# Two heads of K and V in one load: 64 partitions each, rows of 8 KB

## The chip, the core and the metric

The kernel runs on one core of a Trainium2 chip. The metric is device time in microseconds (us), from the start to the end of one execution. Three runs of the kernel before gave 230.35, 232.3 and 233.48 us. The profile that is read below is one more execution; it took 230.15 us, of which its instructions span 228.4 us.

## The reference

Two attention blocks and two feed-forward blocks follow each other, on eight sequences with one new token each. Both attention blocks use the same weights and the same cache; both feed-forward blocks share theirs.

```python
B, Sq, D = 8, 1, 448
Hq, Hkv, Sk, Dh = 16, 8, 4096, 256          # W = 1024: the last quarter of the cache
q = (x @ wq).reshape(B, Sq, Hq, Dh)
scores = einsum("bhqd,bhkd->bhqk", q, k[..., Sk-W:, :]) * Dh ** -0.5   # 2 query heads per K/V head
o = einsum("bhqk,bhkd->bhqd", softmax(scores), v[..., Sk-W:, :])
A(x) = o.reshape(B, Sq, Hq * Dh) @ wo
B(x) = silu(x @ w1) @ w2                     # F = 1792
x = x + A(layernorm(x));  x = x + B(layernorm(x))
x = x + A(layernorm(x));  x = x + B(layernorm(x))
```

All numbers are bf16. For one sequence and one K/V head the window is 1024 positions of 256 numbers, 512 KiB. Over 8 sequences, 8 heads and K and V that is 64 MiB (67.1 MB) of cache, read once and used by both attention blocks. The weights are 10.6 MB.

## The kernel before

All engines are programmed directly. Every piece of work is recorded as a task with what it reads and writes (`Plan.add`); the waits between engines are worked out from that. The order of tasks on PE, DVE, ACT and POOL is not found by the program: it is written out as lists of task numbers (`ORDER`, at the top). SP, which issues nearly all loads, takes its tasks in the order in which the program records them.

**Loads.** The cache goes into 30 slots (`slots`, R = 30), each 128 partitions of 4 KiB: one K or V head. `load_kv` (L490) issues one transfer for one head; the head's 1024 positions are laid out so that partition p holds eight positions in a row, so each of the 128 partitions gets one run of 4 KiB of memory. `pump` (L978) records as many loads as there are free slots; a slot's next load waits until the tasks that last read the slot are done. At the start, SP issues x, the weight of the queries (`wq`, in rows of 8 KiB for its three large parts), the first eight K heads, then `w2` and `wo`, the first eight V heads, `w1`, and then K and V of one sequence after the other. The output leaves in two stores: seven rows for the first seven sequences (L928), and the last row cut in four (L965).

**One sequence, first attention.** DVE turns each K head in place, in 32 by 32 blocks of 4-byte words (`transposes`, L632, run at L639): in one instruction for the first four heads (`WIDE`), in two for the others. `scores` (L642, matmuls at L656) multiplies four heads at once, each on its own 32 rows of PE, for two groups of four heads (`k2`). The query operand `qbd` is spread out over 256 columns for each group: by POOL for the first attention (`q_blocks1`, L626), and by PE and ACT for the second one (L846, L850). `softmax` (L662) takes the maximum (L673), shares it between the row groups (L674, L675, L677), takes the exponential on ACT (L688), rearranges it on PE (L690) and turns it on DVE (L692). `products` (L699, matmuls at L703) multiplies with V head by head, each time with 4 rows fewer, so that each later head overwrites the rows that it owns. The last two heads (`LATE`) are multiplied apart (`products_late`, L712), since their V arrives last. `o_turn` (L725 to L733) scales and turns the result, `wo_rows` (L754) multiplies with `wo`, and `fold` brings the row back into columns.

**The rest of a sequence.** `chain` does the feed-forward block (L544 w1, L818 w2) and the queries of the second attention (L833, L838, L839, L846, L850). `attend2` and `values2` do the second attention from the same slots and so free them. The next sequence's first attention is interleaved with it. The second feed-forward block is done for seven sequences at once in `final_rows`, and for the last one in `final_last`; its helper constants (L874 to L880) are made there. `warm` (L781) puts filler matmuls on PE, whose result nobody reads.

Of the kernel before, what the change touches and what calls it, by code (L numbers as in the profile page):

```python
# [14 lines left out]
        "196 69 74 86 87 88 89 197 198 92 136 94 199 137 138 139 148 149 161 150 200 151 201 154 202 203 157 204 205 "  # L15
        "159 206 207 208 209 228 229 211 213 225 226 231 227 233 235 214 237 215 240 216 242 217 218 248 249 219 275 "
        "276 251 257 220 254 259 264 262 325 277 279 280 278 281 282 221 312 222 313 267 314 315 287 288 223 318 289 "
        "321 290 224 326 327 328 329 323 330 331 343 297 344 333 300 340 341 351 342 346 335 352 353 302 348 354 355 "
        "350 356 357 371 374 376 336 358 409 382 383 368 410 411 385 388 393 391 398 396 412 413 414 415 416 446 447 "
        "448 449 401 337 338 421 452 422 423 424 459 455 339 431 460 461 462 463 434 457 464 465 484 476 477 467 436 "  # L20
        "469 473 474 479 475 481 485 486 483 487 504 509 507 488 489 490 491 515 516 501 542 543 518 521 524 526 531 "
        "529 544 470 546 547 548 549 545 534 579 554 580 581 582 555 556 557 471 585 564 472 588 592 567 593 594 595 "
        "596 590 617 618 597 598 569 609 619 610 600 606 607 612 608 620 621 614 616 602 637 640 642 622 623 675 624 "
        "676 648 649 634 603 604 651 654 657 659 664 662 677 725 679 680 681 682 678 712 713 667 714 715 687 688 689 "
        "718 605 690 721 697 726 727 728 729 730 723 731 742 700 733 743 750 751 752 753 735 739 740 745 741 754 702 "
        "747 755 749 756 757 770 773 775 808 736 767 781 782 809 810 784 787 792 790 797 795 812 813 814 815 811 800 "
        "845 846 847 848 820 821 737 822 851 738 823 854 830 856 859 860 861 833 862 875 863 864 883 876 866 858 884 "
        "885 886 872 887 878 873 874 880 888 882 835 889 903 890 906 908 868 900 941 914 915 942 917 869 920 925 923 "
        "930 928 943 944 945 946 947 948 978 979 980 981 933 870 984 871 953 954 987 955 956 992 993 994 995 989 996 "
        "997 1008 991 963 999 1001 1009 966 1005 1006 1011 1007 1013 1016 1017 1002 1015 968 1018 1036 1041 1039 "  # L30
        "1019 1020 1021 1022 1023 1047 1048 1033 1074 1075 1050 1076 1053 1056 1058 1063 1061 1077 1078 1079 1066 "
        "1080 1081 1084 1085 1086 1087 1105 1106 1107 1108 1090 1111 1118 1093 1003 1004 1114 1142 1143 1144 1119 "
        "1116 1120 1121 1122 1123 1124 1145 1134 1146 1147 1126 1095 1135 1131 1132 1137 1133 1139 1148 1128 1149 "
        "1141 1129 1154 1157 1151 1159 1197 1198 1165 1166 1199 1200 1168 1130 1171 1176 1174 1181 1179 1196 1202 "
        "1250 1224 1184 1225 1226 1227 1237 1238 1239 1240 1211 1208 1233 1251 1246 1252 1253 1235 1254 1259 1248 "
        "1260 1261 1262 1256 1213 1264 1258 1266 1218 1268 1219 1271 1274 1284 1276 1221 1285 1286",
    "dve":
        "37 28 39 43 34 26 36 46 42 25 38 24 5 13 4 54 7 32 44 40 18 30 33 6 22 27 45 50 11 57 31 29 9 49 52 70 15 "
        "19 72 51 73 132 75 58 134 3 84 80 81 59 76 60 141 82 48 135 77 133 10 53 83 140 143 35 16 55 146 144 142 78 "
        "20 17 145 90 91 85 93 14 174 12 21 175 56 147 169 184 185 152 41 170 155 162 163 179 158 160 47 8 189 180 "  # L40
        "190 271 272 236 273 241 243 245 23 247 274 252 309 258 304 310 260 261 311 307 308 306 305 265 266 316 319 "
        "322 295 324 298 301 405 406 407 370 408 375 303 377 379 381 438 441 439 386 442 444 394 392 395 445 443 440 "
        "399 400 450 453 429 456 432 435 458 538 539 503 540 510 508 514 437 512 541 573 571 519 575 576 525 527 528 "
        "574 532 577 572 533 578 583 562 586 565 589 568 591 671 672 570 673 636 674 641 643 645 647 705 706 708 652 "
        "707 711 658 660 661 704 710 709 665 666 716 719 695 722 698 724 701 804 805 703 806 769 807 774 776 778 780 "
        "837 839 838 785 840 842 793 791 794 843 844 798 799 841 849 852 828 855 831 857 834 937 938 939 902 836 940 "
        "907 909 911 913 971 970 973 918 975 977 926 924 927 972 974 976 931 932 982 985 988 961 990 964 967 1070 "
        "1071 1035 1072 1042 1040 969 1046 1044 1073 1098 1100 1051 1099 1101 1057 1059 1060 1097 1064 1065 1103 "
        "1102 1104 1088 1109 1091 1112 1094 1115 1117 1096 1186 1153 1158 1188 1160 1189 1162 1187 1193 1164 1169 "
        "1190 1191 1177 1192 1194 1175 1195 1178 1182 1183 1204 1206 1228 1229 1207 1230 1231 1241 1242 1243 1244 "  # L50
        "1234 1247 1236 1209 1249 1212 1214 1215 1217 1269 1275 1277 1279 1280 1282 1283 1222 1287",
    "act":
        "2 71 164 165 166 167 171 172 176 153 177 168 178 181 182 156 183 186 187 191 188 192 210 212 230 193 232 "
        "234 238 95 173 244 246 250 253 255 263 268 317 320 296 332 299 334 345 347 349 372 378 380 367 384 369 387 "
        "389 397 402 451 454 430 433 466 468 478 480 482 505 513 511 500 517 520 502 522 530 535 584 563 587 566 599 "
        "611 601 613 615 638 644 646 633 650 635 653 655 663 668 717 720 696 699 732 744 734 746 748 771 766 777 779 "
        "783 786 788 768 796 801 850 853 829 832 865 877 867 879 881 904 899 910 912 916 901 919 921 929 934 983 986 "
        "962 998 965 1000 1010 1012 1014 1037 1045 1043 1032 1049 1034 1054 1052 1062 1067 1089 1110 1092 1113 1125 "
        "1127 1136 1138 1140 1150 1155 1152 1161 1163 1167 1201 1170 1172 1180 1203 1205 1185 1232 1245 1255 1263 "
        "1257 1265 1216 1267 1220 1272 1270 1278 1281",  # L60
    "pool":
        "0 1 79 130 131 239 269 270 256 404 403 373 390 536 506 523 537 669 639 656 670 802 772 789 803 905 935 936 "
        "922 1068 1069 1038 1055 1156 1173 1210 1273",
# [160 lines left out]
def bass_interleave_layers__sliding_block_cached__dense_activation_silu__decode_kernel(  # L224
# [5 lines left out]
    H = HD // DH  # L230
# [12 lines left out]
    R = 30  # L243
    WIDE = (0, 1, 2, 3)
    LATE = 2
    WARM = (8, 12, 5, 4, 4, 4, 4, 4, 3)
# [15 lines left out]
    slots = [sb(f"slot{i}", [P, 2048], BF16) for i in range(R)]  # L262
# [43 lines left out]
    def QB(i, k2):  # L306
        return [("qbd", i, k2, q) for q in range(4)]

    PT = [QB(i, 0) for i in range(2)]
    EK = [QB(i, 1) for i in range(2)]  # L310
# [22 lines left out]
    def dma(fn, writes, n_bytes, key, reads=(), rate=407e3, via="sp"):  # L333
# [3 lines left out]
    SCR2 = slots[R - 2][:, :]  # L337
    SCRATCH = {R - 1: ["xrow", "xh", "sq8", "sqh8", "st8", "q1T", "sel", "sel_f", "quad_f", "lsel_f", "nm8", "rh8"] +
               [("sums", "w2", g) for g in range(4)] + [("sums", "wo", g) for g in range(8)], R - 2: ["big8", "junk"]}
# [13 lines left out]
    junk = SCR2[:, 512:512 + D]  # L353

# [19 lines left out]
    const(qbd[1][:], 0.0, [("pad", 1)] + QB(1, 0) + QB(1, 1) + QM, dur=0.2)  # L374
# [17 lines left out]
    for k2 in range(2):  # L392
        dve(lambda e, k2=k2: e.tensor_copy(
            view(perm[:], 8 * (1 - k2), [(32, 4), (2, 4), (1, 2)]),
            view(ident[:], 96 + 8 * (1 - k2), [(1, 4), (-32, 4), (4, 2)])),
            ["ident", "perm0"], [("perm", k2)], 0.12, -1, "init")
    PERM = [("perm", 0), ("perm", 1)]
    for q in range(4):
# [5 lines left out]
        0.2, -1, "init")  # L404
    dve(lambda e: e.tensor_copy(sel_o[:], sel_f.rearrange("p (n a) -> p a n", a=2)), ["sel_f"], ["sel_o"], 0.1, -1,
        "init")
    dve(lambda e: e.tensor_reduce(quad_f, ident[:].rearrange("p (g n) -> p g n", n=4), AX.X, ALU.add), ["ident"],
        ["quad_f"], 0.2, -1, "init")
    dve(lambda e: e.tensor_copy(quad[:].rearrange("p (g n) -> p g n", n=4), quad_f.unsqueeze(2).broadcast_to([P, 32, 4])),
        ["quad_f"], ["quad"], 0.2, -1, "init")  # L410
# [79 lines left out]
    def slot_key(s):  # L490
        return [("slot", s, 0), ("slot", s, 1)]
# [129 lines left out]
    def qdata(i, k2):  # L621
        return view(qbd[i][:], 8 + 256 * k2, [(8, 32), (4, 2), (1, 4)])
# [354 lines left out]
    def pump():  # L977
        while n_load[0] < len(seq) and (n_load[0] < cap[0] or n_load[0] >= R and seq[n_load[0] - R] in freed):  # L978
# [4 lines left out]
            if x == (0, "k", 7):  # L983
                load_w2()
                load_wo()
# [113 lines left out]
```

## Time and profile before

| What | Value |
|---|---|
| Median of three runs | 232.3 us (230.35 to 233.48) |
| The profiled execution, its time and its span | 230.15 us, 228.4 us |
| PE, DVE, ACT, POOL busy | 173.0, 157.2, 71.4, 22.8 us |
| All transfers | 78.21 MB in 22,681 packets, mean 342 GB/s |
| Of these, the queue that SP issues to | 22,486 packets, 77.32 MB |
| Loads of K and of V | 64 and 64, of 512 KB each |
| Median from issue to landing, K and V | 8.3 and 10.1 us |
| Clock granted to PE | full throughout |

The page shows the busy time by engine, then the span cut in 40 slices (a digit is the busy share of a slice in tenths), the transfers, the chain of work that ended last, and the costliest groups of instructions by line. The DMA rows give the mean busy share of the core's 16 DMA engines and the rate that they moved. A "packet" is one run of bytes that a DMA engine moved, or the small write by which it reports that its part of a transfer has ended.

### The profile page before, as it was taken

Reading aid. Unit: us, or ns where it says so; the run is one execution under the profiler, and the core shown is the slowest. Engines: PE = TensorE matmul, PEld = TensorE weight load, DVE = VectorE, ACT = ScalarE, POOL = GpSimd, SP = SyncE. Lnnn points to the kernel's source line nnn. Section 1 sums busy time; section 2 is a strip of 40 time slices with the busy share of each in tenths; the row PEclk is TensorE's granted clock in tenths of the full one; section 3 lists DMA queues with packets and bytes.
Section 4 is the critical chain, followed back from the end, with each engine's and each line's share of the span. In section 5 each row is a group of like instructions: output and inputs, shape, how many; then the busy total and the mean of one; then the engine's idle time right before and its main releaser. Section 6 shows DMA issues by size and latency. Waiting matters only on the chain.

```text
span 228.4 us, 8452 instructions
## 1 busy us (share of the span) xinstructions
PE 173.0 (76%) x3779; PEld 94.1 (41%) x3779; DVE 157.2 (69%) x369; ACT 71.4 (31%) x218; POOL 22.8 (10%) x41
## 2 busy tenths in 40 slices
PE   0020737357878989999898987888989999999894
PEld 0010623123444455445444644554445445544662
DVE  6238989878792797389459837974895589314644
ACT  2000080633302341432324142414332431353341
POOL 1000130000200210101010101110120200000020
PEclk9999999999999999999999999999999999999999
DMA  6999999999999999999999999999999999700000
GB/s 175 413 406 407 382 380 395 411 414 417 405 400 369 377 408 403 396 408 407 406 406 408 402 378 411 408 392 395 410 409 385 380 408 406 307 3 3 0 6 1
DMA packets 22681, 78.21 MB, mean 342 GB/s; under 512 B 2279, under 2 KB 5302, under 8 KB 22262
## 3 DMA queue, kind: packets, MB, share of 16 engines
q1 hardware_dynamic: 22486, 77.32, 86.6%
q8 instruction: 29, 0.48, 0.9%
q10 hardware_dynamic: 160, 0.36, 0.6%
q14 instruction: 6, 0.05, 0.1%
HBM read 77.67 MB, written 0.01 MB: 340 GB/s over the span
## 4 chain that ended last, share of the span: by engine, by line
PE 46%; DVE 31%; DMA 10%; ACT 6%; issue 4%; SPq 2%; DVEq 0%; ACTq 0%
DVE slot L639 12%; DMA slot<-in_A_k_cache_dram 10%; PE bank L656 10%; PE bank L703 7%; DVE slot L472 7%; PE pair L754 6%; PE bank L781 2%; PE pair L833 2%; ACT ot L760 2%; PE bank L675 2%; PE bank L846 2%; PE bank L712 2%; PE bank L833 2%; PE pair L529 2%; PE pair L818 1%
## 5 line engine op out<-in xcount | busy, mean ns | idle before, releaser
L639 DVE STREAM_TRANSPOSE slot<-slot 128x512 uint32<-128x512 uint32 (+1 forms) x96 | 80.2, 866 | 7.0 <-DMA slot<-in_A_k_cache_dram 6.8
L656 PE MATMUL bank<-slot,qbd 128*16 128x256 bf16 (+1 forms) x1024 | 40.9, 285 | 5.1 <-DVE slot L639 2.0
L703 PE MATMUL bank<-slot,qbd 128*24 128x512 bf16 (+6 forms) x416 | 31.1, 393 | 3.5 <-DVE qbd L692 3.3
L656 PEld LDWEIGHTS bank<-slot,qbd 128*16 128x16 bf16 (+1 forms) x1024 | 23.2, 87 | 16.7 <-ACT qbd L850 4.0
L781 PE MATMUL bank<-wq_sb,cols 128*1 128x512 bf16 x192 | 19.6, 416 | 13.9 <-DMA wq_sb<-in_A_wq_dram 13.9
L776 POOL TENSOR_TENSOR fcols<-fcols 128x1 f32<-128x1 f32 x17 | 9.4, 554 | 106.4 <-ACT fcols L774 94.5
L754 PE MATMUL pair<-wo_sb,q1s 128*1 128x449 bf16 x288 | 17.2, 353 | 1.1 <-DVE wo_sb L475 0.8
L850 ACT ACTIVATE qbd<-bank 128x256 bf16<-128x256 f32 x16 | 6.1, 384 | 33.5 <-PE bank L846 33.5
L725 ACT ACTIVATE ot<-bank,q1s 128x512 bf16<-128x512 f32 (+1 forms) x16 | 10.8, 673 | 16.4 <-PE bank L703 11.1
L626 POOL TENSOR_TENSOR qbd<-q1s,fcols 128x256 bf16<-128x256 bf16 x16 | 9.7, 614 | 59.7 <-PE bank L712 42.4
L703 PEld LDWEIGHTS bank<-slot,qbd 128*24 128x24 bf16 (+6 forms) x416 | 9.7, 92 | 11.1 <-DVE qbd L692 4.2
L692 DVE STREAM_TRANSPOSE qbd<-bank 128x256 bf16<-128x256 bf16 x17 | 8.0, 473 | 8.2 <-PE bank L690 7.9
L673 DVE TENSOR_REDUCE q1s<-bank 128x1 f32<-128x256 f32 x15 | 6.3, 423 | 8.1 <-PE bank L656 8.0
L472 DVE TENSOR_REDUCE slot<-wo_sb 128x6 f32<-128x2688 bf16 x4 | 11.8, 2948 | 0.1
L781 PEld LDWEIGHTS bank<-wq_sb,cols 128*1 128x1 bf16 x192 | 4.2, 82 | 15.4 <-issue 13.9
L674 ACT ACTIVATE q1s<-fcols,q1s 128x4 f32<-128x4 f32 x15 | 4.4, 296 | 18.7 <-DVE q1s L673 18.7
L675 PE MATMUL bank<-q1s,quad 128*128 128x4 f32 x30 | 6.0, 269 | 4.7 <-ACT q1s L674 4.5
L598 PE MATMUL pair<-slot,wq_sb 128*128 128x16 bf16 x128 | 3.6, 174 | 7.5 <-DVE slot L591 7.5
L833 PE MATMUL pair<-wq_sb,q1s 128*1 128x256 bf16 x256 | 8.9, 275 | 0.3 <-DVE q1s L765 0.3
L688 ACT ACTIVATE qbd<-bank,q1s 128x256 bf16<-128x256 f32 x15 | 7.1, 472 | 6.3 <-DVE q1s L677 6.0
L712 PE MATMUL bank<-slot,qbd 128*7 128x256 bf16 (+7 forms) x192 | 8.6, 283 | 0.6 <-DVE qbd L692 0.6
L833 PE MATMUL bank<-wq_sb,q1s 128*1 128x512 bf16 x128 | 8.8, 390 | 0.0
(168 smaller groups left out, 244.6 us busy)
## 6 DMA issues: line engine op xcount, KB each, us to landing
slot<-in_A_k_cache_dram SPq DMA_DIRECT2D x64, 512.0 KB, 8.3
slot<-in_A_v_cache_dram SPq DMA_DIRECT2D x64, 512.0 KB, 10.1
wo_sb<-in_A_wo_dram SPq DMA_DIRECT2D x4, 896.0 KB, 14.6
wq_sb<-in_A_wq_dram SPq DMA_DIRECT2D x3, 1024.0 KB, 8.0
w_sb<-in_B_w_dram SPq DMA_DIRECT2D x1, 1568.0 KB, 19.8
w_sb<-in_B_w_dram SPq DMA_DIRECT2D x1, 1344.0 KB, 17.2
wq_sb<-in_A_wq_dram ACTq DMA_DIRECT2D x1, 256.0 KB, 3.5
wq_sb<-in_A_wq_dram SPq DMA_DIRECT2D x1, 256.0 KB, 4.1
```

Source lines behind the costliest of these rows:

```text
L472: dve(lambda e, rows=rows, s=s: e.tensor_reduce(s, rows[:, :, R0:M1].rearrange("p c (a n) -> p c a n", a=2), AX.X, ALU.add, negate=True), ...
L626: pool(lambda e, k2=k2: e.tensor_tensor(qdata(0, k2), q1s[:, b, 64 * k2:64 * k2 + 64].rearrange("p (n r) -> p n r", r=2).unsqueeze(3) .bro ...
L639: dve(lambda e, v=v: e.transpose(v, v), keys, keys, 0.15 + n / 2 / 950, b, ("KW%d" if n > 1024 else "KT%d") % k)
L656: fns.append(lambda e, w=w, j=j, kv=kv, cb=cb, par=par: e.matmul(sc[32 * j:32 * j + up_to, 0:256], w, kv, start=(cb == 0 and par == 0), st ...
L675: pe(lambda e: e.matmul(mx, quad[:], mq, start=True, stop=True, skip_group_check=True), [K[4], "quad"], bk(LB[n]), 0.2, b, "mx%d" % L)
L703: pe([lambda e, t=t: e.matmul(bank[ob][32 * t:32 * t + m, :], pT_sb[L][:, 64 * t:64 * t + m], v[:, 512 * t:512 * t + 512], start=True, sto ...
L712: pe([lambda e, t=t, a=a: e.matmul(o[32 * t:32 * t + m, :], pT_sb[n][:, 64 * t + a:64 * t + a + m], v[:, 512 * t + DH * a:512 * t + DH * a ...
L725: act(lambda e: e.activation(o_t, src[1], ACTF.Copy, scale=sm[b][:, 4 * L + 3:4 * L + 4]), bk(src[0]) + [("sm", b, L, 3)], okey, 0.62, b, ...
L754: fns.append(lambda e, i=i, w=w, c0=c0: e.matmul(bank[XB][32 * (i % 4):32 * (i % 4) + 1, c0:c0 + D + 1], oT[:, oT_col(i):oT_col(i) + 1], w ...
L776: pool(lambda e: e.tensor_tensor(rhalf, var4, nhalf, ALU.pow), ["var4", "nhalf"], ["rhalf"], 0.54, b, "pow" + name)
L781: pe([lambda e, i=i: e.matmul(bank[OB[0]][32 * i:32 * i + 1, :], zero_b, wq_sb[:, 512 * i:512 * i + 512], start=True, stop=True, tile_posi ...
L833: pe([lambda e, j=j, c=c, qh=qh, k2=k2, h=h, n=n: e.matmul(qh[32 * j:32 * j + 1, :], xbt[b][:, xcol(c, k2):xcol(c, k2) + 1], view(wq_sb[:] ...
```

## The change

K and V heads are loaded in pairs. A slot is now 128 partitions of 8 KiB, and there are 15; head 2j lies on partitions 0 to 63, head 2j + 1 on partitions 64 to 127, and each partition holds sixteen positions of its head in one run of 8 KiB. One transfer of 1 MiB fills a slot. Its source is written as a pattern of its own with three dimensions, slowest first: 2 heads (one head's cache apart), 64 rows, 4096 numbers. The last V pair of the last sequence comes in two transfers, each with one half of every row.

What follows from the layout: `qbd` needs 128 columns for a group instead of 256; the scores of one head pair come from two halves of a slot; the constants that share the maximum and rearrange the exponentials change (`perm`, `quad`, `sel4`, `lsel`); `products` accumulates over the two halves of a slot, with 8 rows fewer from pair to pair. The number of turns, score matmuls and product matmuls stays the same. The initial queries are spread by one set of 16 matmuls and two DVE copies instead of 32 matmuls, a DVE and an ACT copy. In the last sequence's second attention, the maximum is shared through PE as in the other sequences instead of by two turns on DVE; the constants of `final_rows` are made in the second sequence; `final_last` scales by the layernorm's factor at the end rather than before w2. All four `ORDER` lists are new.

```diff
...
-    R = 30
-    WIDE = (0, 1, 2, 3)
+    R = 15
+    NP = HKV // 2
+    WIDE = (0, 1)
     LATE = 2
+    SLOT = 4096
...
-    slots = [sb(f"slot{i}", [P, 2048], BF16) for i in range(R)]
+    slots = [sb(f"slot{i}", [P, SLOT], BF16) for i in range(R)]
...
-    def load_kv(s, cache, b, kvh):
+    def load_kv(s, cache, b, j, apart):
+
         extra = SCRATCH[s] if s in SCRATCH and s not in first_use else []
         first_use.add(s)
-        dma(lambda e: e.dma_start(slots[s][:, :].rearrange("p (u d) -> p u d", d=DH),
-                                  cache[b, kvh, S0:SK, :].rearrange("(p u) d -> p u d", p=P)),
-            slot_key(s) + extra, W * DH * 2, "slot%d" % s)
+        a = cache[b, 2 * j, S0:SK, :]
+        step = SLOT // 2 if apart else SLOT
+        for h in range(SLOT // step):
+            src = bass.AP(a.tensor, a.offset + h * step, [[SK * DH, 2], [SLOT, 64], [1, step]])
+            dma(lambda e, h=h, src=src: e.dma_start(slots[s][:, h * step:(h + 1) * step], src),
+                slot_key(s, h if apart else None) + extra, P * step * 2, "last%d" % h if apart else "slot%d" % s,
+                rate=407e3 if apart else 417.7e3)
...
     def qdata(i, k2):
-        return view(qbd[i][:], 8 + 256 * k2, [(8, 32), (4, 2), (1, 4)])
+        return view(qbd[i][:], 8 + 128 * k2, [(8, 16), (4, 2), (1, 4)])
...
-                    a = 16 + 256 * k2 + (j * 8 + cb * 2 + par) * 8
+                    a = 16 + 128 * k2 + (j // 2 * 8 + cb * 2 + par) * 8
                     w = q[:, a - up_to:a]
-                    kv = slots[slot_of[b, "k", 4 * k2 + j]][:, :].rearrange(
+                    kv = slots[slot_of[b, "k", 2 * k2 + j // 2]][:, 2048 * (j % 2):2048 * (j % 2) + 2048].rearrange(
                         "p (u cb jj par) -> p cb par u jj", u=8, cb=4, par=2)[:, cb, par, :, :]
...
+        dve(lambda e: e.tensor_reduce(mneg, x, AX.X, ALU.max, negate=True), bk(sb), [K[0]], 0.41, b, "max%d" % L)
         if part is None:
             act(lambda e: e.activation(mq, sel4, ACTF.Copy, scale=mneg), [K[0], "sel4"], [K[4]], 0.2, b, "mq%d" % L)
...
         else:
...
-            dve(lambda e: e.transpose(mt, mt), [("mt", n)], [("mt", n)], 0.21, b, "mT")
...
+            dve(lambda e: e.tensor_scalar(mq, sel4, mneg, None, op0=ALU.mult), [K[0], "sel4"], [K[4]], 0.12, b, "mqd")
+        pe(lambda e: e.matmul(mx, quad[:], mq, start=True, stop=True, skip_group_check=True), [K[4]] + QUAD,
+           bk(LB[n]), 0.2, b, "mx%d" % L)
...
-    def products(b, L, kvh, ob):
+    def products(b, L, j, ob):
 
-        v = slots[slot_of[b, "v", kvh]]
-        m = 4 * (HKV - kvh)
-        pe([lambda e, t=t: e.matmul(bank[ob][32 * t:32 * t + m, :], pT_sb[L][:, 64 * t:64 * t + m],
-                                    v[:, 512 * t:512 * t + 512], start=True, stop=True, tile_position=(0, 32 * t),
-                                    skip_group_check=True) for t in range(4)],
-           slot_key(slot_of[b, "v", kvh]) + PT[L], bk(ob), 0.055, b, "PV%d" % L)
+        v = slots[slot_of[b, "v", j]]
+        m = 8 * (NP - j)
+        for h in range(2):
+            pe([lambda e, t=t, h=h: e.matmul(
+                bank[ob][32 * t:32 * t + m, :], pT_sb[L][:, 64 * t + 32 * h:64 * t + 32 * h + m],
+                v[:, 2048 * h + 512 * t:2048 * h + 512 * t + 512], start=(h == 0), stop=(h == 1),
+                tile_position=(0, 32 * t), skip_group_check=True) for t in range(4)],
+               slot_key(slot_of[b, "v", j], h) + PT[L], bk(ob), 0.055, b, "PV%d" % L)
...
-            qs = bank[lb][:, 256:512]
+            qs = bank[lb][:, 256:384]
...
-            act(lambda e, qs=qs, k2=k2: e.activation(qbd[1][:, 8 + 256 * k2:264 + 256 * k2], qs, ACTF.Copy), bk(lb),
-                QB(1, k2) + QM * k2, 0.42, b, "qbd%d" % k2)
+            act(lambda e, qs=qs, k2=k2: e.activation(qbd[1][:, 8 + 128 * k2:136 + 128 * k2], qs, ACTF.Copy), bk(lb),
+                QB(1, k2), 0.28, b, "qbd%d" % k2)
...
-    seq = [(b, t, k) for b in range(NB) for t in "kv" for k in range(8)]
+    seq = [(b, t, k) for b in range(NB) for t in "kv" for k in range(NP)]
     n_load = [0]
-    cap = [R - 2]
+    cap = [R - 1]
...
-            freed.update((b, "k", 4 * k2 + j) for j in range(4))
+            freed.update((b, "k", 2 * k2 + j) for j in range(2))
             pump()
...
-            for kvh in range(HKV):
-                products(b, 1, kvh, OB[1])
-                freed.add((b, "v", kvh))
+            for j in range(NP):
+                products(b, 1, j, OB[1])
+                freed.add((b, "v", j))
             pump()
```

## The prediction

> **What bounds the kernel now.** I read the page's slices first, for the transfers.
>
> ```profile
> DMA  6999999999999999999999999999999999700000
> GB/s 175 413 406 407 382 380 395 411 414 417 405 400 369 377 408 403 396 408 407 406 406 408 402 378 411 408 392 395 410 409 385 380 408 406 307 3 3 0 6 1
> DMA packets 22681, 78.21 MB, mean 342 GB/s; under 512 B 2279, under 2 KB 5302, under 8 KB 22262
> ```
>
> The 16 DMA engines are at 90% or more from slice 2 to slice 34, that is from about 6 to 195 us; then they stop, and the last 28 us are work on data that is there. So two things set the time: the stream of 67.1 MB of K and V, and the tail behind its last load. Next I read the waits and the chain, to see whether the engines' work is far from the stream.
>
> ```profile
> SPq L496 <- PE bank L656: 59.5, 12, 8.9
> ...
> DVE slot L639 <- DMA slot<-in_A_k_cache_dram: 6.8, 9, 1.8
> ```
>
> SP waits 59.5 us in all for slots that the score matmuls still hold, at most 8.9 us at a time, and DVE waits only 6.8 us in all for K. Loads and work are nearly balanced, about 21 us for a sequence (67.1 MB / 8 at 408 GB/s is 20.6 us). Work that gets shorter gains little alone; transfers that get slower are seen at once, since they have no reserve.
>
> Then I looked at stretches of the start (columns: length, busy time of PE, PEld, DVE, ACT, POOL, the clock, the DMA engines' share, GB/s). From 6 to 12.5 us nearly all packets are rows of 8 KiB, those of `wq`; from 14 to 22 us they are mostly K in rows of 4 KiB.
>
> ```profile
> 6.00:12.50 6.50, 0.00 (x0) 0.00 (x0) 1.25 (x10) 0.00 (x0) 0.00 (x0) 1.00 1.00 417
> 14.00:22.00 8.00, 1.28 (x21) 0.68 (x17) 6.29 (x21) 0.23 (x1) 0.00 (x0) 1.00 1.03 408
> ...
> 150.00:190.00 40.00, 36.06 (x806) 19.83 (x810) 28.60 (x60) 13.97 (x42) 4.59 (x8) 1.00 1.02 397
> ```
>
> So rows of 8 KiB move at 417 GB/s instead of 408: one engine's sixteenth is 26.1 instead of 25.5 GB/s, 314 ns for a row of 8 KiB and 161 ns for one of 4 KiB. That is what the longer rows can bring, if all 16 engines carry them.
>
> Do they? The new source pattern is written slowest dimension first as 2 x 64 x 4096; so far each load's pattern began with 128 or 64 rows on both sides. The trace has three transfers that begin with fewer than 16: x (8 rows), and the stores of 7 and of 4 rows. I read the packets of the first 2.0 us and of 226.3 to 228.4 us, where only these three run:
>
> ```profile
> DMA packets 16, 0.01 MB, mean 4 GB/s; under 512 B 8, under 2 KB 16, under 8 KB 16
> ...
> DMA packets 22, 0.01 MB, mean 3 GB/s; under 512 B 15, under 2 KB 22, under 8 KB 22
> ```
>
> x has 8 rows of 896 B and just 8 small packets beside them. The stores have 7 rows of 896 B, 4 rows of 224 B, and 11 small packets: 7 + 4. The whole page says the same: 141 loads with 64 or 128 rows at 16 reports each are 2,256, plus 8 + 7 + 4, plus the four rows of 224 B, is 2,279, the page's count under 512 B to the last one. With 16 reports for every transfer it would be 2,308. So a transfer is cut along its outermost dimension into shares that report singly, 16 of them at most, and with fewer rows only so many. Cut that way, a source that begins with 2 makes two shares, and a load of 1 MiB runs on two DMA engines, 512 KiB (64 rows of 8 KiB) on each.
>
> In the three short transfers both sides begin with the same number; here the source begins with 2 and the slot with 128, and no row shows which decides. I take the smaller: a cut in more shares than 2 would have to go through the source's second dimension. The Trainium skill ("DMA: Bandwidth & Descriptors", "Why a DMA increments its semaphore by 16 and not by 1") says that the engines are the largest number up to 16 that divides the outermost counts of both sides, which is 2 here, and that they are then the lowest-numbered ones, load after load; for 8, 7 and 4 the trace agrees, for 2 against 128 no run so far shows it. By that page's 27 GiB/s for an engine, 33.55 MB on each of two would take an estimated 1157 us, and my sum below would be about 1220.
>
> **The sum.** Each of two engines carries 63 loads x 64 rows of 8 KiB, 4,032 x 314 ns = 1267 us, and of the last pair, loaded in halves of a row, 2 x 64 rows of 4 KiB, 128 x 161 ns = 20.6 us: 1288 us. The weights (10.6 MB) still go over all 16, and these two carry their sixteenth, 0.66 MB, in the same order: at 23.8 GB/s (slices 4 and 5, 382 and 380 GB/s) 28 us. Before the first of it 3 us pass. Behind the last load the tail stays: the last V head's first matmul is at 200.68 us, the span ends at 228.4, so 28 us. The execution is 1.75 us longer than its span (230.15 against 228.4). 1288 + 28 + 3 + 28 + 2 = **1349 us**. The profiled execution is 1% below the median of 232.3 us, which does not matter at this size; a difference under about 2% can't be told from no change here.
>
> Both ends: the stream's slowest long stretch, 397 GB/s, gives 24.8 GB/s for an engine, 33.55 MB / 24.8 = 1353 and 1414 in all. Two engines alone may each be faster than a sixteenth of what 16 move together; the nearest row is the best single microsecond of the `wq` loads (10 to 11 us), 451 GB/s or 28.2 for one, hence 1190 and 1251 in all. I take 26.1, the row with the same row length.
>
> Could anything starve the two engines further? A load takes 20 us, a pair of K is turned and used in a few us, and SP is up to 15 loads ahead; a slot that waits for its sequence to end has others queued before it. So nothing else counts but the tail.
>
> **The other edits**, each with its cover. For a sequence, 161 us of loading stand beside some 21 us of work, so all of it is hidden but for the tail; the prices without that cover matter to the first rival.
> - DVE's turns (L639, 64 x 683 and 32 x 1234 ns) keep number and shape. Product matmuls (L703) keep their number, and cost 392 to 399 ns with 12 to 32 rows alike: 0.
> - `qbd` at 128 columns: POOL (L626, 614 ns x 16) was waited for only 1.5 us in all by PE. ACT (L850) goes from 384 ns to somewhere between 178 (128x8, L733) and 384, PE's spread (L846) from 227 ns for 64 columns to between 167 (one column, L529) and 227. Taken at the middle, 0.1 + 4 x 0.03 us, 16 times: 3.5 us, of which PE's idle time for L850 (4.0 us in all) lets perhaps 1 us through.
> - Setup: six more copies of 0.18 us on DVE, which is free from 8 to 14 us (PE first has `wq` at 13.9); 16 fewer q matmuls (189 ns overlapped, 0.6 us for 16) and no ACT copy: -0.6 us once.
> - Ten small DVE operations for `final_rows` (0.06 to 0.17 us, some 1.2 us) move into the second sequence, where DVE is at 70 to 90%: at most +1.2, and they leave a stretch (201 to 211 us) in which DVE was mostly idle: 0.
> - Tail: the maximum by PE costs 0.15 + 0.39 + 0.16 us instead of 0.21 + 0.19 + 0.21 (+0.1), the two L801 of 0.22 us go, one lies on the path (-0.2), and ACT's new copy runs beside PE's w1 matmuls: 0 in all. What would be late next there is PE at L959, which waits for the same tanh.
> - SP issues 65 loads instead of 128 at 0.43 us (L496); a pattern with three dimensions may cost 0.3 (L928) to 0.6 (L965). Queued behind them in SP are only more loads and, at the end, the two stores; at one issue in 20 us nobody waits.
>
> **Rivals.**
> 1. *All 16 engines carry each load* (the slot's 128 partitions decide the cut; the point from which it turns is that the smaller count does not rule). Then 67.1 MB take 160.9 us at 417 instead of 164.5 at 408: -3.6, and -1 from `qbd` and setup: 230.15 - 4.6 = 225.5 us, 221 to 234 with what the new orders may lose or gain. For it: slices at 408 are full, so a faster row would show. Against it: the count of reports. The Trainium skill's "Rules for kernel authors" on the same page asks for 1 MiB and 128 partitions per transfer for most bandwidth, which speaks for this one; the 417 GB/s row agrees for `wq`, whose pattern begins with 128. 12%: 7 faster, 5 within 2%.
> 2. *Two engines for a load, but other ones for the next.* Eight loads in flight then fill all 16; each takes 20.6 us (64 x 314 ns, and its report) instead of 1.3. The first K and the last V come 19 us later: 230 + 2 x 19, less what overlaps, about 260 us. For it speaks only that the page has no view by engine. 4%.
> 3. *16 engines, but the larger slots starve the stream.* A slot is free only when both heads are done; half a slot is 1.29 us at 408 GB/s, and 16 phases of K or V would lose up to 20 us, about 240 us taken at half. Against it: waits of up to 8.9 us for slots left the DMA row full. 2%.
>
> **How the numbers follow.** Two engines: 82%. Its bounds, 1250 to 1415, hold nearly all of it, about 8 in 10 of everything, so the range ends there and leaves the rivals out. Slower by over 2%: 82 + 4 + 2 = 88%; within 2%: 5%; faster: 7%.
>
> **What will show it.** Right: a DMA row with 1 (two of 16 busy is 0.13), about 52 GB/s in nearly all slices; some 65 x 14 = 910 fewer small packets than 16 reports a load would make; K's time to landing of 100 us or more; PE and DVE at 10 to 20% and waiting for loads; a tail of some 28 us. Wrong at its first step if the DMA row stays at 9 and 417 GB/s; wrong in size if two engines alone move clearly more or less than 52 GB/s.

## The result

The changed kernel takes **1339.93 us** (median of four runs, 1338.72 to 1341.01) where the kernel before took 231.57 us beside it (230.35 to 233.48): **5.78 times as long** (95% interval 5.74 to 5.83). The profiled execution took 1338.72 us, its span 1336.9 us. Some executions of a kernel are a few per cent slower than its others: the medians below count them all, the ratios with their intervals only the fast ones, and the profiles of the runs with 16 first, with two transfers for a slot and with 14 slots are of slow ones.

The page's slices of the kernel after, each now 33 us long, and its count of packets:

```profile
PE   0103021120221201121022201022021020113007
...
PEclk9999995565555656655565655555565565556558
DMA  4152121111111111111111111111111111111110
GB/s 150 53 151 86 56 84 53 53 53 53 53 53 53 53 53 53 53 53 53 53 53 54 53 52 53 53 53 53 52 53 53 53 53 53 53 53 53 53 53 6
DMA packets 12699, 78.20 MB, mean 58 GB/s; under 512 B 361, under 2 KB 3384, under 8 KB 4216
```

The 16 DMA engines, at 9 tenths before, show 1 and 53 GB/s from the seventh slice to the last but one. The higher slices at the start hold the weights. The 361 small packets add up to the last one: 65 K and V loads with 2 reports each are 130, the 13 weight loads with 16 are 208, x and the two stores 8 + 7 + 4 = 19, and the four rows of 224 B.

Three stretches (columns: length, busy time of PE, PEld, DVE, ACT, POOL, the clock granted to PE, the DMA engines' share, GB/s):

```profile
14.00:22.00 8.00, 0.60 (x4) 0.12 (x4) 0.00 (x0) 0.00 (x0) 0.00 (x0) 1.00 0.13 53
200.00:700.00 500.00, 81.04 (x1250) 36.48 (x1247) 48.27 (x101) 19.84 (x62) 5.93 (x13) 0.55 0.13 53
...
1310.00:1337.00 27.00, 23.24 (x581) 13.62 (x573) 9.86 (x36) 9.25 (x31) 3.14 (x4) 0.98 0.01 3
```

A share of 0.13 is two of sixteen, from the first K load (14 to 22 us, 408 GB/s before) to the last V, but for the weights. Only the last 27 us are dense work again. The waits of the same kernel (in all, times, longest) say who pays: DVE waited 6.8 us for K before and now 756.2, and PE 319.9 for V.

```profile
DVE slot L662 <- DMA slot<-in_A_k_cache_dram: 756.2, 31, 89.5
...
PE bank L719 <- DMA slot<-in_A_v_cache_dram: 319.9, 21, 18.8
```

### The profile page after: what moved, and what is told of

It is laid out like the page before. It is cut to its first block, busy times and chain, and to the rows that moved or that the text cites. A ratio compares the mean times of both kernels' runs of the same rounds, so it can differ in the third digit from the quotient of the medians.

```text
span 1336.9 us, 8373 instructions
## 1 busy us (share of the span) xinstructions
PE 233.1 (17%) x3767; PEld 109.0 (8%) x3767; DVE 157.1 (12%) x375; ACT 69.9 (5%) x218; POOL 19.3 (1%) x41
## 4 chain that ended last, share of the span: by engine, by line
another core or an unknown queue 66%; SPq 13%; PE 8%; DMA 7%; DVE 4%; issue 1%; ACT 1%; POOL 0%; DVEq 0%
SPq L517 8%; DMA slot<-in_A_k_cache_dram 4%; DMA slot<-in_A_v_cache_dram 3%; DVE slot L662 3%; PE bank L679 2%; SPq L464 2%; SPq L470 1%; SPq L458 1%; PE bank L719 1%; PE pair L845 0%; PE pair L565 0%; PE bank L700 0%; PE bank L799 0%; PE bank L858 0%
## 5 line engine op out<-in xcount | busy, mean ns | idle before, releaser
L662 DVE STREAM_TRANSPOSE slot<-slot 128x512 uint32<-128x512 uint32 (+1 forms) x96 | 80.7, 871 | 756.3 <-DMA slot<-in_A_k_cache_dram 756.2
L719 PE MATMUL bank<-slot,qbd 128*24 128x512 bf16 (+3 forms) x416 | 49.8, 555 | 319.9 <-DMA slot<-in_A_v_cache_dram 319.9
L679 PE MATMUL bank<-slot,qbd 128*16 128x256 bf16 (+1 forms) x1024 | 50.4, 346 | 5.6 <-DVE slot L662 3.2
L730 PE MATMUL bank<-slot,qbd 128*7 128x256 bf16 (+3 forms) x192 | 11.2, 362 | 209.1 <-DMA slot<-in_A_v_cache_dram 209.1
L719 PEld LDWEIGHTS bank<-slot,qbd 128*24 128x24 bf16 (+3 forms) x416 | 10.6, 110 | 338.2 <-DMA slot<-in_A_v_cache_dram 322.7
L772 PE MATMUL pair<-wo_sb,q1s 128*1 128x449 bf16 x288 | 23.3, 467 | 0.9 <-ACT q1s L751 0.8
L858 PE MATMUL bank<-qbd,band 128*128 128x32 bf16 x64 | 5.8, 226 | 97.5 <-DVE qbd L851 63.1
L830 PE MATMUL pair<-w_sb,q1s 128*1 128x449 bf16 x112 | 12.1, 516 | 33.2 <-DVE q1s L818 31.8
L845 PE MATMUL pair<-wq_sb,q1s 128*1 128x256 bf16 x256 | 14.4, 392 | 14.8 <-DVE q1s L783 14.8
L648 POOL TENSOR_TENSOR qbd<-q1s,fcols 128x128 bf16<-128x128 bf16 x16 | 6.3, 398 | 547.4 <-PE bank L730 374.1
L845 PE MATMUL bank<-wq_sb,q1s 128*1 128x512 bf16 x128 | 14.1, 585 | 0.0
```

Source lines behind the costliest of these rows:

```text
L662: dve(lambda e, v=v: e.transpose(v, v), keys, keys, 0.15 + (i1 - i0) * 512 / 950, b, ("KW%d" if i1 - i0 > 1 else "KT%d") % (2 * j + h))
L679: fns.append(lambda e, w=w, j=j, kv=kv, cb=cb, par=par: e.matmul(sc[32 * j:32 * j + up_to, 0:256], w, kv, start=(cb == 0 and par == 0), st ...
L719: pe([lambda e, t=t, h=h: e.matmul(bank[ob][32 * t:32 * t + m, :], pT_sb[L][:, 64 * t + 32 * h:64 * t + 32 * h + m], v[:, 2048 * h + 512 * ...
L730: pe([lambda e, t=t, a=a, h=h: e.matmul(o[32 * t:32 * t + m, :], pT_sb[n][:, 64 * t + 32 * h + a:64 * t + 32 * h + a + m], v[:, 2048 * h + ...
L772: fns.append(lambda e, i=i, w=w, c0=c0: e.matmul(bank[XB][32 * (i % 4):32 * (i % 4) + 1, c0:c0 + D + 1], oT[:, oT_col(i):oT_col(i) + 1], w ...
L830: fns.append(lambda e, f=f, w=w, c0=c0: e.matmul(bank[XB][32 * (f % 4):32 * (f % 4) + 1, c0:c0 + D + 1], hT[b][:, f:f + 1], w, start=(f < ...
```

## Experiments

The theory on record: a transfer is cut along its outermost dimension, so a source that begins with 2 puts each load on two DMA engines, always the same ones. The runs first vary that number in the kernel before, then ask what the same bytes cost when they are ordered otherwise. A time is a median, and its ratio is to runs of the kernel before on the same chip.

### The number that stands first, in the kernel before

```diff
-  slots[s][:, :].rearrange("p (u d) -> p u d", d=DH),
-  cache[b, kvh, S0:SK, :].rearrange("(p u) d -> p u d", p=P)
+  slots[s][:, :],                      # N = 2, 8, 16, and later 32
+  bass.AP(..., [[2048, N], [2048 * N, P // N], [1, 2048]])
```

**2 first.** 

> The kernel before, with one thing changed: partition p no longer holds rows 8p to 8p+7 of its head, but the 128 rows of 4 KiB are dealt out between the two halves of the partitions, so that the source pattern begins with 2 (2 x 64 x 2048). K and V alike, so the result is the same; sizes, slots, orders and work stay. Theory (a load is cut along the source's outermost count): two engines carry everything, 8192 rows x 155 to 161 ns on each = 1270 to 1320 us, plus weights, start and tail of some 60: 1330 to 1380 us, DMA row at 1, 50 to 53 GB/s. Rival (what is slow is the pair: heads 2 MiB apart, transfers of 1 MiB, rows of 8 KiB, fewer slots): about 232 us, since nothing of that is here.

Measured: 1360.23 us (one run; 232.2 us before). Its slices and packets:

```profile
DMA  4152121111111111111111111111111111111110
GB/s 147 52 147 87 52 86 52 52 53 52 52 53 52 52 53 52 53 53 52 52 52 52 53 52 52 52 52 52 52 52 53 52 52 52 52 53 52 52 52 6
DMA packets 20889, 78.20 MB, mean 58 GB/s; under 512 B 487, under 2 KB 3510, under 8 KB 20470
```

One edit to the order in which a load's rows are written down turns the kernel before into the changed one's time: rows of 4 KiB, one head, work and orders as before. So neither the pairs nor the 8 KiB rows nor the new orders are behind the 1340 us. The second rival, other engines for the next load, falls with the kernel after (start, length, both in us):

```profile
4.02 45.54 SPq L517 DMA_DIRECT2D slot<-in_A_k_cache_dram  x4
```

By 49.6 us SP had issued four pairs, 4.2 MB, of which 53 GB/s can have moved 2.4 MB at most. So more than one load was under way, and still the share was 0.13 and the rate 53 GB/s: the loads queued on the same two engines.

**8 first.** 

> The same with the source pattern 8 x 16 x 2048. Theory: eight engines, 2048 rows x 157 to 161 ns on each = 322 to 330 us, plus some 60 = 380 to 395 us, DMA row at 5, about 205 GB/s. Rival (any pattern with three dimensions, or rows that do not follow each other in memory, is slow by itself): as slow as with 2, over 1300 us, or independent of the count.

Measured: 412.21 us (one run). The DMA row is at 5 and the rate of nearly all later slices at 204 to 211 GB/s, four times that of 2 first; the slope is the theory's. It is 4% over the expected range; slices 2 to 5 (10 to 51 us), with weights and K together, have 132 to 204 GB/s. I did not separate that.

**16 first.** 

> The same with the source pattern 16 x 8 x 2048. Theory: all 16 engines again, 227 to 237 us, no difference from before, DMA row at 9. Rival (the pattern's three dimensions, or rows of 4 KiB that lie 64 KiB apart, cost by themselves): over 245 us.

Measured: 318.08 us (314.32 to 337.91), ratio 1.354 (1.340 to 1.368). A miss:

```profile
DMA  7999999999999999999999999999999999980000
GB/s 239 351 235 251 381 315 246 250 283 259 263 275 267 268 265 260 262 262 266 266 273 279 283 283 278 273 274 265 266 275 265 261 250 250 251 217 1 4 2 3
DMA packets 22681, 78.21 MB, mean 243 GB/s; under 512 B 2279, under 2 KB 5302, under 8 KB 22262
```

The packets are those of the kernel before, number for number (2279 small ones), and all 16 engines are at 9. But in most slices they move 250 to 283 GB/s where the kernel before had 400. So a full DMA row is not yet full speed: the same packets each take longer. The number of engines is not the whole story.

### Two transfers for a slot of the changed kernel

```diff
-  src = bass.AP(..., [[SK * DH, 2], [SLOT, 64], [1, step]]);  dst = slots[s][:, ...]
+  for g in range(2):                   # one head each
+      src = bass.AP(..., offset + g * SK * DH, [[SLOT, 64], [1, step]])
+      dst = slots[s][64 * g:64 * g + 64, ...]
```

> The changed kernel, with one thing changed: each slot is filled by two transfers, one for each head, from patterns that begin with 64 rows of 8 KiB (the last pair by four). Layout, work and orders are those of the changed kernel. Theory: the pattern's outermost count of 2 was the whole loss; with 16 engines the first rival of the prediction holds, 225 us, 221 to 234, DMA row at 9 and 415 to 418 GB/s in full slices, 314 ns or less for a row of 8 KiB. Rival (pairs, larger slots or new orders lose by themselves): over 240 us, with SP waiting for slots and a DMA row below 9.

Measured: 353.16 us (341.27 to 356.55). A quarter of the changed kernel's time, with the same computation, and still far from the 225.5 us of my first rival. The DMA row is full, and the rate is 206 GB/s from 14 to 22 us, 222 from 60 to 100, and up to 269 in a later slice.

### What makes packets slow on 16 busy engines

Three runs take this apart. 32 first, again in the kernel before:

> The kernel before with the source of each load written as 32 x 4 x 2048, rows dealt out as in the runs with 2, 8 and 16 first; nothing else changed. Two explanations of the slow packets with 16 first (254 ns for a row of 4 KiB instead of 160, all 16 engines busy) are open. (a) Where the shares lie in the slot: with 16 first, each engine writes 8 neighbouring partitions, and with 128 first it writes others; the sharing out over partitions is taken to follow the count that stands first. With 32 it may be that of 128 again (then 227 to 237 us and some 400 GB/s), or again neighbours (then 300 to 330). (b) The order in which rows of memory are read (neighbouring partitions get rows that are 128 KiB apart, here 64 KiB, wherever they go), or the third dimension of the pattern: then this run is as slow as the one with 16 first, 300 to 330 us, and rates of 250 to 285 GB/s. A time below 240 us rules (b) out.

Measured: 236.57 us (234.17 to 237.64), ratio 1.015 (1.008 to 1.023). Between 16 and 32 first the slowness goes, but for some 1.5%, though rows that are neighbours in the slot still come from far apart in memory and the pattern still has three dimensions. That leaves (a), where in the slot each engine's share lies, by elimination.

Two transfers for a head in the kernel before, first by halves of the slot, then by even and odd partitions (the edits in outline):

```diff
+  for g in range(2):
+      slots[s][64 * g:64 * g + 64, :]  <-  rows 64 * g to 64 * g + 63            # halves
+      partitions g, g + 2, g + 4, ...  <-  rows g, g + 2, g + 4, ...             # even and odd
```

Halves: 

> The kernel before with each load of a head cut into two transfers, one for partitions 0 to 63 and one for 64 to 127; rows of 4 KiB, memory read in the same order, patterns of two dimensions, the same slots and the same computation. It separates what the run with two transfers for a slot (353 us) had together: transfers onto half of the partitions on one side, rows of 8 KiB from two heads 2 MiB apart and the pairs' slots on the other. If a transfer onto 64 neighbouring partitions is slow by itself, the DMA row is full, the rate 215 to 285 GB/s and the time 290 to 360 us. If the two heads or the 8 KiB rows were the cause, the rate stays near 400 GB/s and the time is 228 to 245 us. Small packets under 512 B rise by 128 x 16 to 4327 either way.

Even and odd: 

> The kernel before with each head loaded by two transfers of 64 partitions and rows of 4 KiB, as in the run with partitions 0 to 63 and 64 to 127 (328.9 us), but one for the even and one for the odd partitions; every row goes to the partition that it has in the kernel before, so the computation is unchanged. If what makes the packets slow is where the 64 partitions lie (one side of the slot at a time), this run goes at some 400 GB/s and takes 228 to 245 us. If it is the smaller transfer, or 64 rows to 16 engines, it is as slow as that run, 300 to 350 us.

Measured: halves 328.9 us (326.83 to 351.32), ratio 1.413 (1.399 to 1.427); even and odd 244.75 us (243.98 to 247.34), ratio 1.060 (1.052 to 1.068). The stretches of the halves:

```profile
14.00:22.00 8.00, 1.39 (x21) 0.79 (x21) 3.54 (x10) 0.23 (x1) 0.00 (x0) 1.00 1.03 230
60.00:100.00 40.00, 24.50 (x384) 10.57 (x388) 15.24 (x31) 6.46 (x20) 2.26 (x4) 0.69 1.03 248
```

and of the even and odd partitions:

```profile
14.00:22.00 8.00, 1.34 (x21) 0.71 (x20) 6.24 (x21) 0.23 (x1) 0.00 (x0) 1.00 1.03 409
60.00:100.00 40.00, 34.30 (x739) 17.48 (x741) 24.50 (x54) 11.70 (x36) 3.46 (x6) 1.00 0.98 353
```

Same number of transfers, rows, bytes, and a share of 1.03 in both first lines: 230 GB/s onto 64 neighbouring partitions, 409 onto every second one. So the place of the partitions makes some 82 of the 96 us by which the halves are longer than the kernel before, and neither rows of 8 KiB nor two heads are needed for it. The other 14 us, with 353 GB/s at a nearly full row later on, remain in the even and odd run; whether they come with smaller transfers, with twice as many of them or with partitions that are not neighbours, I did not separate.

The Trainium skill has a rule that orders these three ("SBUF — State Buffer", "Door 1: The DMA port swizzle (why `[64,N]` ≈ `[32,N]`)"): 128 partitions are reached through 16 ports, partitions 0 to 63 through only eight of them, and, by its table of ports, the even partitions through all. By it a half runs at half of 408, an estimated 204 GB/s. The pair in two transfers begins there, with 206, and rises to 269; the halves move 230 to 289, which is 13 to 42% more than the estimate. So the order agrees and the size only in part; what makes the rate rise, no run shows. The same page ("Can I just issue two DMAs to hit both halves?") says that a second transfer for the other half does not help; both runs agree. Which engine wrote which partitions in the run with 16 first, no trace here shows.

### The same pairs, 64 rows first

```diff
-  src = bass.AP(..., [[SK * DH, 2], [SLOT, 64], [1, step]])
+  src = bass.AP(..., [[SLOT, 64], [SK * DH, 2], [1, step]])
```

> The changed kernel with the two outer dimensions of the load's source swapped: 64 rows first, then 2 heads, then 4096 numbers. The same bytes of memory go into the same slots in rows of 8 KiB with as many transfers; only which partition gets which row differs (the two heads alternate from partition to partition), and what the scores and products make of it is left as it is, so this kernel computes something else and is run for its time alone. If the leading 2 of the source was all that kept the load on two engines, 16 engines carry each load, small packets under 512 B come to 65 x 16 + 13 x 16 + 19 + 4 = 1271, and the time is the first rival's: 225.5 us, 221 to 234. If the slowness of the run with 16 x 8 x 2048 (318 us) comes with any source of three dimensions, or with rows of two heads 2 MiB apart read at the same time, the DMA row is full but the rate 215 to 285 GB/s, and the time is 290 to 360 us. If the larger slots starve the stream (third rival), the DMA row has gaps and the time is about 240 us.

Measured: **234.94 us** (232.88 to 239.56, ten runs), ratio 1.008 (1.003 to 1.012). Swapping two entries of one list takes 1105 us off (in a kernel whose heads then alternate from partition to partition, so that its result is another one). Its slices:

```profile
DMA  6999999999999999999999899969998999800000
GB/s 164 422 407 417 380 382 414 420 419 423 423 392 346 410 423 372 420 419 381 296 424 422 358 361 422 423 267 405 413 424 332 347 355 388 327 3 3 3 3 4
DMA packets 13609, 78.20 MB, mean 335 GB/s; under 512 B 1271, under 2 KB 4294, under 8 KB 5126
```

and two stretches and a wait of it, with the second stretch of the kernel before between them:

```profile
14.00:22.00 8.00, 1.10 (x28) 0.64 (x24) 4.46 (x19) 0.00 (x0) 0.00 (x0) 1.00 1.02 422
...
150.00:200.00 50.00, 43.64 (x958) 23.56 (x962) 35.21 (x80) 14.68 (x47) 4.30 (x9) 0.97 0.94 371
```

```profile
150.00:200.00 50.00, 45.35 (x999) 25.05 (x1003) 34.56 (x74) 16.70 (x51) 4.59 (x8) 1.00 0.99 386
```

```profile
DVE slot L662 <- DMA slot<-in_A_k_cache_dram: 21.1, 12, 6.9
```

The longer rows do what the first rival said of them: 422 GB/s instead of 408 while nothing else limits. But the time is 9.4 us above that rival's 225.5, and no gain. From 150 to 200 us the share is 0.94 and the rate 371, where the kernel before, whose last load is issued some 6 us sooner, has 0.99 and 386 (1.02 and 397 from 150 to 190 us, the figures that the prediction and the next expectation take): the row has gaps, and DVE waits three times as long for K. The next runs ask first for the slots, and then for the work. (Scores and products for heads that alternate were not written, and the two halves were not tried on two queues.)

### 1 MiB of slots less in both

```diff
-    R = 15        (changed kernel, 64 rows first)      -    R = 30        (kernel before)
+    R = 14                                             +    R = 28
```

The order lists stay the same, with the loads left out of their numbering, here and in the last two runs.

14 slots of 8 KiB: 

> The changed kernel with the load's source 64 rows first (234.9 us; its partitions get other rows, so it computes something else), and 14 slots instead of 15. It tests why that run took 9 us more than the 225.5 of my first rival although its rows of 8 KiB moved at 422 GB/s from 14 to 22 us: from 150 to 200 us the DMA share was 0.94 where the kernel before had 1.02. If loads come late because slots come free late (the third rival), a slot less is 1 MiB less ahead, 2.5 us at 417 GB/s, for each of the phases in which SP waits: 238 to 255 us. If the slots are not what holds the stream back, 233 to 237 us.

28 slots of 4 KiB: 

> The kernel before with 28 slots of 4 KiB instead of 30, so as many bytes less as in the run with 14 slots of 8 KiB. SP waits for slots here too, 8.9 us at most, but the DMA row stayed full, so there is some reserve: if it is as large as the row suggests, 230 to 235 us; if slots are short here as well, as much more as the run with 14 slots loses against 15.

Measured: 249.45 us (248.07 to 253.51), ratio 1.076 (1.068 to 1.084), and 248.81 us (247.72 to 249.49), ratio 1.075 (1.068 to 1.081). Here are their 150 to 200 us, first 14 slots of 8 KiB, then 28 of 4 KiB:

```profile
150.00:200.00 50.00, 41.07 (x814) 20.50 (x810) 30.15 (x66) 13.38 (x42) 3.74 (x8) 0.91 0.85 320
```

```profile
150.00:200.00 50.00, 43.19 (x868) 21.96 (x857) 32.19 (x64) 15.11 (x46) 5.76 (x10) 0.93 0.91 353
```

I had read a reserve out of the full row of the kernel before, and expected 230 to 235 us of it. There is none: two slots fewer cost it 7.5%, about what one large slot costs the other (from 1.008 to 1.076). Slots hold the loads back in both, so this does not tell the two apart.

### The work without later loads

```diff
     def load_kv(...):
+        if s in first_use:
+            return
```

Kernel before: 

> The kernel before with each slot loaded once: K and V of the first sequence and 14 heads of the second are loaded as ever, all later work takes what lies in the slots. So 98 of 128 loads are left out, and the result is another one; the work on the engines keeps its number and order. It gives the time that the work takes when no load holds it up after some 65 us (26 MB of weights and first heads at 408 GB/s). If the stream sets the time of the kernel before, as my prediction had it (waits of DVE for K were 6.8 us in all, PE idle 13% from 60 to 195 us), the time falls by more than 10 us, to 205 to 220. If work and stream are equally long, as the loss of 17 us with 28 slots suggests, it falls by less: 221 to 230 us.

Changed kernel, 64 rows first: 

> The changed kernel with the load's source 64 rows first (234.9 us), each slot loaded once, as in the run beside it: 15 of 64 pairs are loaded. Against that run it tells what the rest of the change (pairs, narrower spread of the queries, new orders, setup, tail) does to the work alone. My first rival counted 1 us less for it (3.6 us more for the longer rows). If so, it takes some 1 us less than the kernel before with one fill. If the new orders or the pairs cost work, it takes more; by 5 us or more, that explains why 16 engines and longer rows gave 234.9 instead of 225.5 us. If both take the same and are well below their full kernels, the gain of the longer rows went to loads that start late, since slots come free late.

Measured: 230.12 us (228.53 to 232.79), ratio 0.994 (0.989 to 0.998), and **225.52 us** (225.11 to 225.93), ratio 0.974 (0.970 to 0.979). The slices of the first one, and then of the second:

```profile
PE   0020736357878989989888988888899999999894
...
DMA  6999999999991000000000000000000000000000
```

```profile
PE   0012417277689998989899899888988989999994
...
DMA  6999999999991000000000000000000000000000
```

The kernel before gains 1.9 us when three quarters of its K and V loads are gone. Behind the first loads, its work alone takes nearly as long as work and stream together; PE is at 7 to 9 without any load to wait for. And the work of the changed kernel is 4.6 us shorter than that of the kernel before, of which its 15 first loads, at 422 instead of 408 GB/s, can make an estimated 1.3 us. Loads then cost it some 8 us (from 0.974 to 1.008 of the kernel before), against 1.4 there (from 0.994 to 1). That loads start later when slots come free by pairs would explain it, and DVE's wait for K (10.1 us in the run without later loads, 21.1 with them) points the same way; but I have no run with pairs loaded and heads freed singly, so that cause is argued, not shown.

## Why the prediction was right

**The cut.** The step that carried all, that the source's leading 2 decides and not the slot's 128, is shown twice: by the reports (361 small packets) and by the runs that change nothing but the number that stands first (2 first in the kernel before, 1360 us; 64 first in the changed one, 234.9 us). In all these runs the smaller count is the source's, so that the smaller one decides, and not simply the source's, stays argued. The Trainium skill's rule that the prediction cited ("DMA: Bandwidth & Descriptors", "Why a DMA increments its semaphore by 16 and not by 1") agrees for 2 against 128, for 8 and for 64. That they are the lowest-numbered engines no view here shows; that they are the same ones for load after load, the 53 GB/s with more than one load under way do.

**The sum**, term by term. The kernel after, from 200 to 700 us:

```profile
DMA packets 3284, 26.57 MB, mean 53 GB/s; under 512 B 50, under 2 KB 50, under 8 KB 50
```

| Term | Predicted, us | Measured, us |
|---|---|---|
| A row of 8 KiB on one engine | 0.314 | 0.309 (500 us x 2 engines / 3234 rows: 3284 packets less 50 small ones) |
| 4,032 rows | 1267 | 1246 (4,032 x 0.309) |
| last pair, 128 rows of 4 KiB | 20.6 | not separate; 20.6 kept |
| weights on the two engines, start | 28 + 3 | 41, the rest up to the last V's first matmul at 1308.0 |
| tail | 28 | 28.9 (1308.0 to 1336.9) |
| outside the span | 2 | 1.8 |
| Sum | 1349 | 1338.7 |

The rows were 1.6% cheaper than 16 engines' common rate says, and the start and weights, with whatever else the remainder holds, 10 us dearer; the two, 21 us less and 10 us more, partly cancel, and neither end of my range was needed. The Trainium skill's rate, an estimated 1157 us for the stream, would have been too short: one engine moved 8192 B in 309 ns, 26.5 GB/s.

**Starvation.** I held that SP is up to 15 loads ahead and that nothing but the tail counts. The second half stood, the first did not. SP's issues of the kernel after (duration in ns, min / median / max, first and last start in us):

```profile
L517 SPq DMA_DIRECT2D slot<-in_A_v_cache_dram x33: 1413/19492/36838, 99.3 to 1264.3; - x33
L517 SPq DMA_DIRECT2D slot<-in_A_k_cache_dram x32: 523/19492/24790, 4.0 to 1163.8; - x32
```

An issue that took 0.43 us before holds SP for 19.5 us, as long as a load takes. So SP is never far ahead, and everything behind it waits too: `w2` is issued only at 49.6 us, though 14 of 16 engines have had nothing to do since about 14 us, and the first V at 99.3. I had priced what is queued behind the loads at nothing, since an issue would take at most 0.6 us. By the sum it cost some 10 us at most, little beside so long a stream.

**The other edits** were costed for the first rival, and there I was wrong in two sizes. The rest of the change was to bring 1 us; in the work alone it is 4.6 us (230.12 to 225.52), or some 3 us without the quicker first loads. `qbd` brought what was said of it: POOL's spread (L648) went from 614 to 398 ns and ACT's copy (L862, L850 before) from 384 to 277 ns with 64 rows first. Which of the orders, the setup and the tail brought the rest, I did not separate. And the 3.6 us of the faster rows were counted in full, because I took the stream to set the time of the kernel before. The step that failed there is "loads and work are nearly balanced" read as "the stream binds": the work alone takes 230 us, so that a faster stream had 1.9 us to give at most.

**The rivals.** The first fell as a forecast; with 64 rows first, its price came out at 234.9 instead of 225.5 us, just above its 221 to 234. The second fell with the first four loads of the kernel after. The third, that larger slots starve the stream at about 240 us, was given 2%; with 16 engines the gaps in the DMA row were there.

**The signs.** Small packets fell by 1918, from 2279 to 361. My 910 were meant against 65 loads with 16 reports each, and 1271 - 361 = 910 is just what the run with 64 rows first has more. The landing time of K and V, which I expected at 100 us or more, is missing on the page: with two reports for a load it shows no landing at all.

```profile
slot<-in_A_k_cache_dram SPq DMA_DIRECT2D x32, 1024.0 KB
slot<-in_A_v_cache_dram SPq DMA_DIRECT2D x31, 1024.0 KB
```

## What to carry to other kernels

Before a source pattern is written by hand, look at the number that stands first on both sides: 2 first put 1 MiB on two engines and took 1340 us, 64 first took 235, with the same bytes into the same slots, though onto other partitions; counting the small packets of a trace against its loads shows such a cut. A DMA row of 9 is full speed only if the GB/s beside it say so, for the same 16 engines moved 230 GB/s onto half of a slot's partitions and 409 onto every second one. And whether a stream or the work sets the time is not read from a full DMA row: leave the later loads out once, and see what is left.

## What was not expected of the hardware

- **Issue is held by a transfer on few engines.** SP's issue took a median of 19.5 us with 2 first and 8 KiB rows, 9.9 us in the run with 2 first and 4 KiB rows, and 2.3 us with 8 first, in each case about the time that the load itself takes.
- **The granted clock fell on a mostly idle PE, but not at once.** In the first 200 us PE was busy for 22 us, and the clock stayed full. From 200 to 700 us, with PE busy a sixth of the time, it was 0.55; over the whole kernel the 128 x 512 products took 555 ns in the mean instead of 393. In the tail, with PE busy again, it was 0.98, and the tail took 28.9 us, 27.7 before. What brings the clock down, no run here separates. It cost nothing here, since the loads beside it ran on at 53 GB/s throughout.
- **16 engines can be busy and slow.** 4 KiB rows at a share of 1.03 moved 236 GB/s in the run with 16 first from 14 to 22 us, against 408 in the kernel before.
